# A fused agent attention and soft mixture of experts on one core: the expert layers in half tiles, with a new order of all steps

## The chip, the cores and the metric

The kernel runs on one core of a Trainium2 chip. The metric is the device time of one execution in microseconds (us), the median of several runs. A profile of one execution gives the trace that is read here; the engines in it are TensorE (PE, with its weight loads as PEld), VectorE (DVE), ScalarE (ACT), GpSimd (POOL) and the queue that issues the transfers (SP).

## The reference

Everything is float32. Attention comes first: four batches of 11456 tokens with 128 channels, and 49 agents in each batch.

```python
a2k = softmax(scale * agents @ k.T);  agent_v = a2k @ v
q2a = softmax(scale * q @ agents.T);  x = q2a @ agent_v        # 45824 x 128 over all batches
logits = x @ phi                                               # 32 slots: 8 experts x 4
d = softmax over the tokens of logits;  slot_input = d.T @ x   # 32 x 128
for e in range(8):                                             # w1: 128 x 1024, w2: 1024 x 128
    slot_out[e] = relu(slot_input[e] @ w1[e]) @ w2[e]          # 4 x 128
c = softmax over the slots of logits;  out = c @ slot_out      # 45824 x 128
```

The expert layers work on 32 rows in all, but no output can be formed before they are done, since the softmax over the tokens needs every logit.

## The kernel before

The work has three stages. In the load stage q, k and v stream in from device memory in tiles of about 1 MB (`qx`, `kx`, `kv` issue them); TensorE forms the scores (`ks`, `qs`), the agents' values (`kE`), transposes (`qp`) and logits (`ql`), and the other engines do the softmaxes. The logits of all tokens stay on the chip in `x_all`. In the middle stage the slots' inputs are completed (`ea` to `l4`), and the expert layers run (`mh`, `mr`, `mt`, `mc`, `mo`), then the sum over experts and its division (`ms`, `sb`, `sd`), which leave `sob`. In the output stage 25 chunks of the softmax over the slots are multiplied with `sob` (`oo`), copied out of the accumulators (`va` on VectorE, `vb` on ScalarE) and stored (`od`). A chunk's softmax before that is a row maximum (`cr`, VectorE), a subtraction (`cu`, GpSimd), an exponential (`ce`, ScalarE), a sum (`os`, VectorE), a small addition (`oe`, ScalarE), a reciprocal (`or`, VectorE), a product (`om`, GpSimd) and a transposition (`ot`, VectorE). These need only the logits, so they fill VectorE's time in the middle stage.

The order of all 1281 steps is one list written out by hand (`ORDER`). Each engine runs its steps in the order in which they stand in it, and the SP queue issues the transfers in that order. A step may be put anywhere behind what it depends on.

The weights `w1` (4 MB, `w10` to `w13`) and `w2` (4 MB, `w20` to `w23`) come in as eight transfers of 1 MB. Seven of them need memory that is free only once the last `kE` step (`kE23`) has read its tile; `w22` uses a buffer of the q tiles, and ORDER has it between `kv21` and `kv22`.

The first expert layer (`m_h`, L786): `si[:, e, :]` holds expert e's four slots in columns 4e to 4e+3 of 32 columns, zeros elsewhere. Experts 0 to 3 (`eh` 0) and 4 to 7 (`eh` 1) have a tile each; expert 4eh+j is written to the rows 32j to 32j+31, so that four products run side by side in four column groups of the array. Of the 32 rows of a block 4 hold values. `m_relu`, `m_trans` and `m_copy` then handle 128 x 512 for each half `fh` of each tile: four of each, 16 transposes in all. `m_out` (L816) is 64 products of 128 columns. `m_so` copies 128 x 128, and `m_sb` adds the four blocks with one product.

Of the kernel before, what the change touches and what calls it, by code (L numbers as in the profile page):

```python
# [47 lines left out]
wu qx0 qs0.0 qs0.1 kx0 ks0.0 ks0.1 qt0 qm0 qx1 qs1.0 qE0.0 qE0.1 qE0.2 km0 qs1.1 qt1 qx5 qE0.3 qm1
qu1 qs5.0 qs5.1 qt5 qm5 kz0 qw0 qr0 qx2 qs2.0 qs2.1 qt2 qm2 qe1 kb0 kr0 ke0.0 kx1 ks1.0 ks1.1 kp0
qE2.0 km1 kz1 kb1 kr1 qx3 qu5 qe5 qs3.0 qs3.1 ke0.1 kT0 kx2 ks2.0 ks2.1 qf5 kp1 qE2.1 qt3 ke1.0  # L50
ke1.1 qd1 qw1 qm3 kx3 ks3.0 qE2.2 km2 kT1 qN0 qp0.0 qp0.1 kz2 qd5 qE2.3 qc0 qw2 ks3.1 qu3 qe3 kv0
kE0 kA0 kb2 kr2 kp2 qr1 km3 kz3 qr2 ke2.0 ke2.1 kT2 ka1 qx4 qs4.0 qs4.1 qd3 qw3 kb3 qN1 qp1.0
qp1.1 kv1 kr3 kp3 kE1 qN2 ka2 qc1 kx4 ks4.0 ks4.1 ka3 ke3.0 ke3.1 qw5 qr3 qt4 qm4 qE4.0 kx5 ks5.0
kA1 km4 kz4 ks5.1 qE4.1 qE4.2 kT3 kb4 kr4 kp4 ke4.0 kv2 kE2 cx0 qp2.0 qp2.1 kv3 qN3 ke4.1 qp3.0
kA2 kT4 kE3 km5 kz5 kb5 qc2 qp3.1 kr5 am0 ka5 qx6 qs6.0 qs6.1 ke5.0 ka4 qc3 ke5.1 qr5 kA3 kv4 kE4
kv5 kT5 kE5 qx11 qs11.0 qt6 qm6 kA4 kA5 qE4.3 qw4 qr4 kg5.1 kh5.1 kg5.2 kh5.2 kg5.3 kh5.3 qs11.1
qt11 qN5 ql0 qM0 qv0 r20 qx9 qs9.0 qE6.0 qE6.1 qs9.1 qN4 qx7 qs7.0 qs7.1 kx6 qt9 r40 qp4.0 r30 qt7
qm7 qm9 qm11 qE6.2 qE6.3 qw6 r50 qp4.1 qp5.0 qc4 ks6.0 ks6.1 km6 qr6 kz6 ru0.0 qp5.1 qc5 qx8 qs8.0
qs8.1 qt8 ql1 kb6 kr6 ke6.0 ke6.1 kp6 qx10 qs10.0 qs10.1 qm8 qE8.0 qN6 kh5.4 qM1 qv1 r21 qt10
re0.0 qE8.1 ru0.1 qu9 qx12 re0.1 qs12.0 qs12.1 qt12 qE8.2 r41 r31 r51 rg0.0 kT6 kx7 ks7.0 ks7.1  # L60
km7 rg0.1 rc0 qE8.3 qe9 qw8 ru1.1 kz7 cr1 kx8 ks8.0 ks8.1 qp6.0 kb7 kr7 km8 qu7 qe7 qd7 qp6.1 kv6
kE6 qf9 qr8 kz8 ke7.0 ke7.1 qc6 kT7 qw7 qr7 ql2 kp7 kb8 kr8 ke8.0 qN8 kA6 ka7 ke8.1 re1.1 qM2
ru1.0 re1.0 r22 qm10 kx9 ks9.0 ks9.1 r42 kv7 kE7 qm12 qd9 kA7 r32 qN7 qp7.0 qv2 qp7.1 r52 kp8
rg1.0 rg1.1 km9 cr3 qE10.0 qE10.1 kz9 qc7 kv8 qp8.0 ru2.1 qp8.1 qc8 kx10 ks10.0 cu3 qx14 qw9 rc1
# [24 lines left out]
qw20 qu21 qe21 ru7.1 qf21 kE19 qE22.0 kT20 qt24 kb21 kr21 qx19 qr20 ke21.0 ke21.1 ql8 kA19 qs19.0
qs19.1 rg7.0 qd21 qM8 r28 r48 qm24 qv8 qw21 qr21 r38 kx22 kx23 ce6 kp21 qN20 ks22.0 qN21 qz17 qw23  # L90
ks22.1 re7.1 rg7.1 qt19 km22 qr18 r58 ea qE24.0 ka20 rc7 kz22 qp20.0 kT21 qE22.1 qE22.2 kE20 qN18
kA20 kb22 kr22 qm19 ks23.0 ks23.1 cr16 ru8.1 km23 kz23 kv21 ke22.0 ke22.1 kT22 qp20.1 re8.1 kp22
qu19 qc20 qe19 kE21 kb23 kr23 qd19 ke23.0 ke23.1 kT23 qp21.0 ru8.0 qw19 ka23 w22 ka21 kA21 qr19
qp21.1 qc21 cu16 qN19 cu2 cr15 kv22 ka22 qw24 kE22 cr12 kA22 kv23 qE22.3 qw22 kE23 ce4 re8.0 qr24
# [959 lines left out]
```

## Time and profile before

| | us |
|---|---|
| median of 3 runs | 287.17 |
| lowest and highest run | 286.89, 287.3 |
| the profiled execution: its own time | 286.32 |
| its span in the trace | 284.3 |

| engine | busy us | share of the span |
|---|---|---|
| PE | 243.7 | 86% |
| DVE | 221.3 | 78% |
| ACT | 198.6 | 70% |
| POOL | 126.2 | 44% |

A share of busy time is an average over stages with different limits, so the trace is read by stage. 103.82 MB are moved in the span, 79.70 MB read and 23.59 MB written.

### The profile page before, as it was taken

Reading aid. Unit: us, or ns where it says so; the run is one execution under the profiler, and the core shown is the slowest. Engines: PE = TensorE matmul, PEld = TensorE weight load, DVE = VectorE, ACT = ScalarE, POOL = GpSimd, SP = SyncE. Lnnn points to the kernel's source line nnn. Section 1 sums busy time; section 2 is a strip of 40 time slices with the busy share of each in tenths; the row PEclk is TensorE's granted clock in tenths of the full one; section 3 lists DMA queues with packets and bytes.
Section 4 is the critical chain, followed back from the end, with each engine's and each line's share of the span. In section 5 each row is a group of like instructions: output and inputs, shape, how many; then the busy total and the mean of one; then the engine's idle time right before and its main releaser. Section 6 shows DMA issues by size and latency. Waiting matters only on the chain.

```text
span 284.3 us, 8467 instructions
## 1 busy us (share of the span) xinstructions
PE 243.7 (86%) x3370; PEld 130.6 (46%) x3370; DVE 221.3 (78%) x431; ACT 198.6 (70%) x678; POOL 126.2 (44%) x139
## 2 busy tenths in 40 slices
PE   6959889999998999999999999997599878487920
PEld 4213646543564655356664556865437422122200
DVE  0597774699998878999989999988558998686510
ACT  2459696566997876599889888988713597657630
POOL 0034521207565341565752676795602868244100
PEclk9999999999999999999999999999759797668555
DMA  7999999999999999999999999379700299999996
GB/s 251 428 418 418 420 408 416 424 403 416 342 427 419 418 420 419 395 372 417 419 418 420 408 413 411 118 308 425 308 2 2 116 415 420 412 420 425 421 417 279
DMA packets 16454, 103.82 MB, mean 365 GB/s; under 512 B 2080, under 2 KB 2464, under 8 KB 5152
## 3 DMA queue, kind: packets, MB, share of 16 engines
q1 hardware_dynamic: 16272, 103.21, 89.0%
q8 instruction: 26, 0.43, 0.6%
q10 hardware_dynamic: 144, 0.08, 0.1%
q14 instruction: 12, 0.10, 0.1%
HBM read 79.70 MB, written 23.59 MB: 363 GB/s over the span
## 4 chain that ended last, share of the span: by engine, by line
PE 52%; DMA 28%; DVE 8%; ACT 4%; issue 3%; SPq 1%; ACTq 1%; DVEq 0%
PE ev L313 12%; PE sq L236 12%; DMA qt<-qT 10%; DMA out<-ot 10%; PE sk L236 9%; PE tp L470 6%; DMA vt<-vL 4%; DMA kt<-kT 3%; ACT ot L877 3%; PE gp L577 3%; PE lq L520 3%; PE pa L864 2%; PE hp L790 2%; DVE ct L856 1%; DVE cd L838 1%
## 5 line engine op out<-in xcount | busy, mean ns | idle before, releaser
L438 ACT ACTIVATE pt<-pt,mx 128x49 f32<-128x49 f32 x148 | 47.5, 326 | 0.1
L236 PE MATMUL sk<-kt,ag 128*32 128x512 f32 (+1 forms) x384 | 45.8, 570 | 1.6 <-DMA kt<-kT 1.4
L236 PE MATMUL sq<-qt,ag 128*32 128x512 f32 (+3 forms) x400 | 43.8, 554 | 3.8 <-DMA qt<-qT 3.6
L313 PE MATMUL ev<-vt,et 128*64 128x129 f32 x720 | 44.9, 276 | 2.1 <-DMA vt<-vL 1.4
L864 PE MATMUL pa<-ct,sob 32*128 32x512 f32 (+2 forms) x50 | 35.0, 824 | 11.5 <-DVE ct L856 8.0
L877 ACT COPY ot<-pb 128x1536 f32<-128x1536 f32 (+2 forms) x25 | 32.4, 1307 | 17.4 <-DMA out<-ot 9.9
L313 PEld LDWEIGHTS ev<-vt,et 128*64 128x64 f32 x720 | 39.3, 136 | 8.9 <-issue 6.2
L459 POOL TENSOR_TENSOR pt<-pt,rt 128x784 f32<-128x784 f32 (+3 forms) x20 | 27.1, 1355 | 34.6 <-DVE rt L455 26.5
L296 ACT ACTIVATE es<-sk,nm 128x512 f32<-128x512 f32 (+1 forms) x48 | 29.7, 652 | 10.3 <-DVE nm L287 8.2
L864 PE MATMUL pb<-ct,sob 32*128 32x512 f32 (+2 forms) x150 | 36.1, 834 | 0.0
L850 POOL TENSOR_TENSOR x_all<-x_all,cd 128x512 f32<-128x512 f32 (+2 forms) x25 | 23.6, 961 | 24.9 <-DVE cd L845 24.6
L553 POOL TENSOR_TENSOR dt<-x_all,mb 128x512 f32<-128x512 f32 (+1 forms) x20 | 24.2, 1217 | 21.5 <-DVE mb L549 17.7
L306 DVE STREAM_TRANSPOSE et<-es 128x1024 f32<-128x1024 f32 (+1 forms) x24 | 28.0, 1165 | 3.1 <-ACT es L296 3.1
L589 POOL TENSOR_TENSOR x_all<-x_all,r_all 128x512 f32<-128x512 f32 (+3 forms) x25 | 23.8, 963 | 14.1 <-DVE r_all L585 8.5
L475 ACT COPY pT<-tp 128x1024 f32<-128x1024 f32 (+3 forms) x25 | 23.0, 920 | 8.8 <-PE tp L470 8.8
L268 DVE TENSOR_REDUCE mt<-sk 128x2 f32<-128x1024 f32 (+1 forms) x24 | 27.4, 1141 | 1.8 <-PE sk L236 1.5
L438 ACT ACTIVATION_READ_ACCUMULATOR pt<-pt,mx 128x1 f32 x148 | 28.0, 189 | 0.0
L864 PEld LDWEIGHTS pa<-ct,sob 32*128 32x128 f32 x50 | 10.2, 246 | 33.7 <-DVE ct L856 22.1
L874 DVE COPY ot<-pa 128x512 f32<-128x512 f32 (+2 forms) x25 | 15.5, 624 | 12.9 <-DMA out<-ot 9.5
L413 DVE STREAM_TRANSPOSE pt<-sq 128x1024 f32<-128x1024 f32 (+3 forms) x20 | 21.9, 1097 | 2.0 <-PE sq L236 1.5
L236 PEld LDWEIGHTS sq<-qt,ag 128*32 128x32 f32 x400 | 10.9, 109 | 23.4 <-issue 16.7
L470 PE MATMUL tp<-cs,pt 128*128 128x128 f32 x140 | 21.3, 283 | 0.0
(126 smaller groups left out, 421.6 us busy)
## 6 DMA issues: line engine op xcount, KB each, us to landing
out<-ot SPq DMA_DIRECT2D x21, 1024.0 KB, 7.2
vt<-vL SPq DMA_DIRECT2D x20, 1032.0 KB, 11.1
qt<-qT SPq DMA_DIRECT2D x20, 1024.0 KB, 9.4
kt<-kT SPq DMA_DIRECT2D x19, 1024.0 KB, 9.3
w2s<-w SPq DMA_DIRECT2D x4, 1024.0 KB, 9.4
w1s<-w SPq DMA_DIRECT2D x4, 1024.0 KB, 15.1
vt<-vL SPq DMA_DIRECT2D x4, 645.0 KB, 8.3
kt<-kT SPq DMA_DIRECT2D x4, 640.0 KB, 9.1
```

The source lines that it names most:

```text
L236: t_.matmul(sp[32 * q4:32 * q4 + 32, h, :nt], ag[:, b, 32 * h:32 * h + 32], xv[:, q4, :], start=True, stop=True)
L268: v_.tensor_reduce(out=k["mt"][:, 0:2], in_=k["s"][:, :, :nt], axis=AX.X, op=ALU.max, negate=True)
L296: s_.activation(out=k["e"][:, h, :nt], in_=k["s"][:, h, :nt], func=AF.Exp, bias=k["nm"][:, 2 * h:2 * h + 1])
L306: v_.transpose(out=k["et"][:, :n].rearrange("p t (h a) -> p h t a", h=2), in_=k["e"][:, :, :nt].rearrange("p h (t a) -> p h t a", a=32))
L313: t_.matmul(k["ev"][o:o + AW, :], k["et"][:, c, :], k["v"][:, c, :], start=c < 2, stop=c >= n - 2)
L438: s_.activation(out=x, in_=x, func=AF.Exp, bias=q["mx"][:, c:c + 1], accum_out=q["rt"][:, c:c + 1])
L459: g_.tensor_tensor(out=x, in0=x, op=ALU.mult, in1=q["rt"][:, :n].unsqueeze(2).to_broadcast([P, n, A]))
L470: t_.transpose(q["tp"][:, h, j % 4, :], q["pt"][:, 2 * j:2 * j + 2, :].rearrange("p c a -> p (c a)"), ident)
L553: g_.tensor_tensor(out=q["dt"][:, :q["n"]], in0=x_all[:, q["at"]:q["at"] + q["n"]], op=ALU.add, in1=r["mb"].unsqueeze(1).to_broadcast([P, ...
L589: g_.tensor_tensor(out=x_all[:, x], in0=x_all[:, x], op=ALU.subtract, in1=r_all[:, x].unsqueeze(2).to_broadcast([P, q["n"], S]))
L864: t_.matmul(pb[:, r - 1, :32 * n] if r else pa[:, :32 * n], sob[32 * r:32 * r + 32, :], z["ct", j][32 * r:32 * r + 32, :32 * n], start=Tru ...
L877: s_.copy(out=o_ov(j)[:, 1:4], in_=z["pb", j][:, :, :32 * CHUNKS[j]])
```

## The change

All eight experts now go into one tile, in two column ranges of 512 (`fh`) that are taken in quarters of 256 columns (`q`): for each j expert j and expert j+4 are added up in the same 32 rows, where they sit in different rows. Relu, transposes and copies are made on 128 x 256 four times, and there are 8 transposes. In the second layer one product has 256 columns: the second-layer weights of experts j and j+4 side by side. Each row is right in one of the two halves; two masks `sel_e`, made by two ScalarE instructions in `am0`, select it in `m_sb`, which becomes two products. The weights' layout in device memory is changed to match, and `w1`'s two first pieces are all that `mh0` needs, its two last `mh1`. And ORDER is written anew for all steps; what follows shows its stretch around the expert layers.

```diff
 ORDER = """
...
-kA23 os3 qr22 qp18.0 qp18.1 kg23.2 qN24 qN22 kg23.1 kh23.1 os0 kh23.2 qr23 kh23.4 w20 qp19.0 qN23
-rg8.0 eb oe3 kg23.3 kh23.3 qc18 os7 cr13 cr14 cr17 os1 rg8.1 rc8 or3 os2 qp19.1 qc19 oe0 ql10 w21
-w23 cu14 w11 w13 qM10 r210 qp24.0 ec qc24 cu15 ce15 ed ql9 r410 r310 qM9 r29 or0 rx10 ry10.0
-qp22.0 qp22.1 qc22 cu7 cu11 ef r49 r39 eg ce2 ce14 oe2 qv9 ql12 rg10.0 eh qp23.0 r59 ru9.1 cu13
-ry10.1 rg10.1 ru9.0 qz24 om3 ei oe7 qc23 qM12 ce16 r212 os4 oe1 r412 r312 rx12 ql11 or2 qv12 qM11
-r211 r411 r311 nm os8 rc10 re9.1 ce11 re9.0 rx11 dE ej wt rg9.0 rg9.1 rc9 ry11.0 ry11.1 or7 wr ws
-ce10 rg11.0 rg11.1 f0 ry12.0 rc11 rg12.0 rc12 gm qv10 cu17 om2 cu12 ce12 ce13 ce17 l1 l2 ce9 f1 l3
-cr24 f2 l4 os17 ce7 d1 qv11 os9 w10 mh0.0 mh0.1 mr0.0 cr21 cu24 w12 mh1.0 mh1.1 mr1.0 or1 os6 os5
-cu8 mt0.0 mr0.1 mt0.1 oe4 om1 ce24 mr1.1 mt1.0 mt1.1 oe8 mc0.0 om0 ot0 mo0.0 oe5 mc0.1 mc1.0 mc1.1
-d2 cr18 mo0.1 cr19 mo1.0 or4 os14 ot1 or5 ot2 ot3 mo1.1 ms oe6 cu19 ce8 os11 om7 d3 d4 sb sd oo0
...
+kz22 kT21 qs19.1 rg7.0 kb22 kr22 ke22.0 kp22 qE22.1 ka22 rg7.1 ce8 rc7 ks23.0 ea qt19 qm19 kE20
+r58 kA20 cu7 qf21 ke22.1 kv22 qd21 qN20 qN18 ks23.1 qp18.0 qp18.1 kv21 kE21 cr14 km23 kz23 qE22.2
+qw21 kb23 kT22 qr21 ru8.1 kr23 qd23 qu19 ce2 kA21 cr15 qp20.0 qe19 kE22 ke23.0 ke23.1 qN21 kT23
+kv23 kE23 cr12 ka23 qp20.1 qd19 qE22.3 kA22 re8.1 ce6 kA23 ru8.0 qw19 qr19 os0 w11 re8.0 qp21.0
+os3 cr13 qc20 qr24 os5 qw23 kg23.1 rg8.0 rg8.1 qw22 qr22 qr23 os1 kh23.1 rc8 qp21.1 qc21 kg23.3
+kg23.2 kh23.2 kh23.3 qN19 qp19.0 qp19.1 cu15 kh23.4 qN24 qc18 eb ql10 qc19 qp24.0 ec os2 oe3 qc24
+qN22 oe1 qN23 os8 os4 ql9 qM10 r210 r410 ed os7 qp22.0 r310 rx10 qp22.1 qM9 oe2 qc22 ef eg r29 r49
+cu10 ry10.0 or1 qp23.0 qc23 oe8 ry10.1 rg10.0 rg10.1 r39 cu12 ce7 eh qv9 cu13 ce13 r59 ru9.1 ei
+cr16 os10 ql11 qM11 ce12 oe7 rc10 ql12 qM12 r212 r412 r211 cr18 os14 ce9 r312 ru9.0 qz24 r411 r311
+cr19 ce11 re9.0 re9.1 oe0 rx11 rg9.0 nm wt wr oe5 os6 rg9.1 rx12 ry11.0 qv12 ws rc9 oe4 ry11.1
+rg11.0 rg11.1 or8 ry12.0 or5 rg12.0 os11 or2 oe6 cu14 cu16 om8 w12 w20 w21 ce16 rc11 f0 rc12 om1
+om2 oe14 or14 gm l1 f1 or0 om0 l2 or6 w13 om6 cu19 oe11 f2 l3 l4 ce15 ce14 qv10 dE ce10 w23 or4
+qv11 w10 mh0.0 mh0.1 mr0.0 mh1.0 mr0.1 mt0.0 om14 mt0.1 ej mc0.0 cr24 os12 or3 mh1.1 ce19 or7
+mc0.1 d1 mo0 mr1.0 mr1.1 os16 mt1.0 mt1.1 cu18 ot0 cr20 cu20 mc1.0 mc1.1 mo1 os13 w22 mo2 mo3 d2
+ot1 ot2 om5 d3 cr21 cu21 cu24 oe10 ms sb d4 oe13 sd oo0 va0 ce24 om3 ot3 oe16 vb0 od0 os9 oe9 oo1
...
-    so = keep.tile([P, C], F32, name="so")
+    so = keep.tile([P, 2, C], F32, name="so")
+    sel_e = keep.tile([P, 2, P], F32, name="sel_e")
...
     def am():
         s_.mul(out=ag[:, 1:], in_=ag[:, 1:], mul=SCALE)
+        for h in range(2):
+            s_.activation(out=sel_e[:, h], in_=sel_d, func=AF.Copy,
+                          scale=cs[:, CO_EM + h:CO_EM + h + 1])
...
+    def m_h(fh, q):
+        if q == 0:
+            hps[fh] = tile_("s", [P, 2, 512], f"hp_{fh}")
+        for e in range(E):
+            j = e % 4
+            t_.matmul(hps[fh][32 * j:32 * j + 32, q, :256], si[:, e, :],
+                      z["w1"][:, 2 * fh + e // 4, j, q * 256:q * 256 + 256],
+                      start=e < 4, stop=e >= 4)
+
+    def m_relu(fh, q):
+        if q == 0:
+            hss[fh] = tile_("pt", [P, 2, 512], f"hs_{fh}")
+            v_.tensor_scalar(out=hss[fh][:, 0, :256], in0=hps[fh][:, 0, :256], scalar1=0.0,
+                             scalar2=None, op0=ALU.max)
         else:
-            s_.activation(out=hss[eh][:, 1], in_=hps[eh][:, 1], func=AF.Relu)
+            s_.activation(out=hss[fh][:, 1, :256], in_=hps[fh][:, 1, :256], func=AF.Relu)
+
+    def m_trans(fh, q):
+        if q == 0:
+            htp[fh] = tile_("s", [P, 2, 4, P], f"htp_{fh}")
+        for i in range(2):
+            t_.transpose(htp[fh][:, q, i, :], hss[fh][:, q, i * P:(i + 1) * P], ident)
+
+    def m_copy(fh, q):
+        if q == 0:
+            hts[fh] = tile_("pt", [P, 2, 4, P], f"ht_{fh}")
+            s_.copy(out=hts[fh][:, 0, 0:2], in_=htp[fh][:, 0, 0:2])
         else:
-            v_.tensor_copy(out=hts[eh][:, 1], in_=htp[eh][:, 1])
+            v_.tensor_copy(out=hts[fh][:, 1, 0:2], in_=htp[fh][:, 1, 0:2])
+
+    def m_out(x):
+        if not x:
+            z["so"] = tile_("a", [P, 2, C], "so_p")
+        for i in range(2):
             for j in range(4):
+                t_.matmul(z["so"][32 * j:32 * j + 32],
+                          hts[x // 2][:, x % 2, i, 32 * j:32 * j + 32],
+                          w2s[x][:, i, 2 * j:2 * j + 2, :], start=not x + i,
+                          stop=x == 3 and i == 1)
...
     def m_sb():
         z["sb"] = tile_("a", [P, C], "sb_p")
-        t_.matmul(z["sb"], sel_d, so, start=True, stop=True)
+        for h in range(2):
+            t_.matmul(z["sb"], sel_e[:, h], so[:, h], start=not h, stop=h == 1)
...
+        h[fh] = [op("mh", (fh, q), "P", lambda fh=fh, q=q: m_h(fh, q),
+                    deps=[si4] + wx[2 * fh:2 * fh + 2] + ([("mh", fh, 0)] if q else []),
...
+        r = [op("mr", (fh, q), "A" if q else "V", lambda fh=fh, q=q: m_relu(fh, q),
+                deps=h[fh] + ([("mr", fh, 0)] if q else []),
...
+        t[fh] = [op("mt", (fh, q), "P", lambda fh=fh, q=q: m_trans(fh, q),
+                    deps=r + ([("mt", fh, 0)] if q else []),
...
```

The transfers are issued by the new list in the order `kv22 kv21 kv23 w11 w12 w20 w21 w13 w23 w10 w22`; by the old one in the order `kv21 w22 kv22 kv23 w20 w21 w23 w11 w13 w10 w12`.

## Rows read from the trace of the kernel before

**Rows 1.** The page: DMA share in 40 slices of 7.1 us; instruction queue (packets, MB, share)
```profile
DMA  7999999999999999999999999379700299999996
...
q8 instruction: 26, 0.43, 0.6%
```

**Rows 2.** Windows by stage; the header names the columns
```profile
core 0: us, PE busy (x) PEld busy (x) DVE busy (x) ACT busy (x) POOL busy (x), PEclk, DMA share, GB/s
0.00:52.60 52.60, 43.91 (x478) 24.02 (x478) 33.63 (x57) 32.53 (x134) 12.26 (x17) 1.00 0.98 396
52.60:185.00 132.40, 130.27 (x2102) 72.37 (x2103) 121.19 (x223) 109.02 (x444) 70.83 (x73) 1.00 0.97 392
185.00:207.70 22.70, 17.56 (x411) 12.83 (x411) 17.06 (x49) 16.75 (x44) 15.44 (x21) 0.88 0.80 326
207.70:221.80 14.10, 12.59 (x180) 7.00 (x180) 11.06 (x28) 3.56 (x11) 3.54 (x5) 0.82 0.01 2
221.80:284.30 62.50, 39.37 (x200) 14.37 (x200) 38.38 (x79) 36.77 (x47) 24.17 (x25) 0.67 0.92 378
```

**Rows 3.** Timeline of the SP queue, 160 to 200 us: start, duration, line, transfer
```profile
184.99 1.28 SPq L683 DMA_DIRECT2D w2s<-w  x3
186.31 2.33 SPq L678 DMA_DIRECT2D w1s<-w  x4
```

**Rows 4.** The chain that ended last, 203 to 224 us: start, duration, what
```profile
204.14 2.16 issue
206.30 0.63 PE fb L745 x2
...
207.53 0.20 DVE si L765
...
207.77 6.10 PE hp L790 x32
...
213.90 0.69 DVE hs L797
...
216.06 1.23 DVE ht L814 x2
...
220.62 0.18 DVE so L827
...
221.45 0.35 DVE sob L834
```

**Rows 5.** Windows of one us, columns as in rows 2
```profile
205.00:206.00 1.00, 0.00 (x0) 0.00 (x0) 0.00 (x0) 1.00 (x2) 1.00 (x2) 0.50 0.08 33
...
211.00:212.00 1.00, 1.00 (x8) 0.20 (x4) 0.52 (x1) 0.00 (x0) 0.00 (x0) 0.50 0.00 0
212.00:213.00 1.00, 1.00 (x12) 0.32 (x8) 0.77 (x2) 0.79 (x3) 0.00 (x0) 0.66 0.00 0
```

**Rows 6.** Groups by shape, 207 to 222 us: count, busy us, mean ns, idle before
```profile
L838 DVE TENSOR_REDUCE cd<-x_all 128x16 f32<-128x512 f32 x6 | 3.8, 654 | 0.0
L822 PE MATMUL so_p<-w2s,ht 128*32 128x128 f32 x128 | 3.7, 273 | 0.0
...
L806 PE MATMUL htp<-cs,hs 128*128 128x128 f32 x16 | 2.2, 281 | 0.0
...
L797 DVE TENSOR_SCALAR hs<-hp 128x512 f32<-128x512 f32 x2 | 1.4, 692 | 2.9 <-PE hp L790 2.9
L814 DVE COPY ht<-htp 128x512 f32<-128x512 f32 x2 | 1.3, 672 | 0.0
...
L800 ACT ACTIVATE hs<-hp 128x512 f32<-128x512 f32 x2 | 1.2, 597 | 7.7 <-DVE hs L797 7.7
...
L831 PE MATMUL sb_p<-so,cs 128*128 128x128 f32 x2 | 0.5, 326 | 1.0 <-DVE so L827 1.0
...
L827 DVE COPY so<-so_p 128x128 f32<-128x128 f32 x1 | 0.2, 240 | 0.0
```

**Rows 7.** Timeline of VectorE, 183 to 224 us: one transposition of logits
```profile
202.77 1.21 DVE L532 STREAM_TRANSPOSE x_all<-lq 128x1024 f32<-128x1024 f32 x1
```

More of the change, by code (lines that the diff above doesn't have):

```diff
@@ L44 @@
 CO_AB = CO_DD + P
-CO_N = CO_AB + P
+CO_EM = CO_AB + P
+CO_N = CO_EM + 2
 ORDER = """
[L48 to L64, printed above, removed]
@@ L89 @@
[L89 to L94, printed above, removed]
@@ new lines @@
+qp2.0 kv1 qE0.2 qE0.3 qu3 qe3 kp2 kE1 qp2.1 km3 kz3 qw0 qf5 qd5 ke2.1 kT2 qr0 qc2 kb3 qm4 qw1
+qE4.0 kA1 kx4 kr3 kp3 ks4.0 ks4.1 km4 kx5 ks5.0 ks5.1 qN0 kz4 kb4 kr4 ke3.0 kv2 qr1 kE2 ke3.1 kT3
+kp4 cx0 qp0.0 qp0.1 qw5 km5 kA2 kz5 ke4.0 ke4.1 ka4 qN1 qp1.0 kT4 qE4.1 qd3 qw3 ka3 qc0 kv3 kE3
+kA3 qp1.1 kb5 kv4 kE4 qc1 qr3 qx6 kr5 ke5.0 ke5.1 kT5 kA4 kv5 qx11 qN3 qp3.0 am0 qs6.0 qs6.1 kE5
+ka5 qE4.2 qE4.3 qw4 qr4 kA5 qt6 qp3.1 kg5.1 kh5.1 kg5.2 kh5.2 qc3 qs11.0 kg5.3 kh5.3 qm6 qE6.0
+qE6.1 qE6.2 qN4 qs11.1 qt11 ql0 qM0 qx9 r20 qv0 qs9.0 qs9.1 qt9 r40 kx6 ks6.0 r30 qm9 r50 ks6.1
@@ L676, in z_w1 @@
         if "w1" not in z:
-            z["w1"] = wl("w1s", [P, E, F])
-        nc.sync.dma_start(out=z["w1"][:, 2 * x:2 * x + 2, :], in_=w1[x])
+            z["w1"] = wl("w1s", [P, 4, 4, F // 2])
+        nc.sync.dma_start(out=z["w1"][:, x], in_=w1[x])
     def z_w2(x):
-        w2s[x] = (tile_("qt", [P, 2, F // P, C], f"w2s{x}") if x else
-                  wl(f"w2s{x}", [P, 2, F // P, C]))
+        w2s[x] = (tile_("qt", [P, 2, E, C], f"w2s{x}") if x else
+                  wl(f"w2s{x}", [P, 2, E, C]))
         nc.sync.dma_start(out=w2s[x], in_=w2[x])
@@ L784, in z_d4 @@
         s_.copy(out=dr, in_=z["dr"])
-    def m_h(eh, fh):
-        if fh == 0:
-            hps[eh] = tile_("s", [P, 2, 512], f"hp_{eh}")
-        for j in range(4):
-            t_.matmul(hps[eh][32 * j:32 * j + 32, fh, :], si[:, 4 * eh + j, :],
-                      z["w1"][:, 4 * eh + j, fh * 512:fh * 512 + 512], start=True, stop=True)
-    def m_relu(eh, fh):
-        if fh == 0:
-            hss[eh] = tile_("pt", [P, 2, 512], f"hs_{eh}")
-        if fh == 0:
-            v_.tensor_scalar(out=hss[eh][:, 0], in0=hps[eh][:, 0], scalar1=0.0, scalar2=None,
-                             op0=ALU.max)
-        else:
-            s_.activation(out=hss[eh][:, 1], in_=hps[eh][:, 1], func=AF.Relu)
@@ L802, in m_trans @@
-    def m_trans(eh, fh):
-        if fh == 0:
-            htp[eh] = tile_("s", [P, 2, 4, P], f"htp_{eh}")
-        for i in range(4):
-            t_.transpose(htp[eh][:, fh, i, :], hss[eh][:, fh, i * P:(i + 1) * P], ident)
-    def m_copy(eh, fh):
-        if fh == 0:
-            hts[eh] = tile_("pt", [P, 2, 4, P], f"ht_{eh}")
-        if fh == 0:
-            s_.copy(out=hts[eh][:, 0], in_=htp[eh][:, 0])
-        else:
-            v_.tensor_copy(out=hts[eh][:, 1], in_=htp[eh][:, 1])
-    def m_out(eh, fh):
-        if not eh and not fh:
-            z["so"] = tile_("a", [P, C], "so_p")
-        for f in range(4):
+    def m_h(fh, q):
[6 more added lines that the diff above has]
+                      start=e < 4, stop=e >= 4)
@@ L920, in tile_agent_attn_soft_moe @@
     d4 = op("d4", (), "A", z_d4, deps=(d3,), gives=(("a", d3),))
-    mo = None
-    for eh in range(2):
-        h = [op("mh", (eh, fh), "P", lambda eh=eh, fh=fh: m_h(eh, fh),
-                deps=[si4] + wx[2 * eh:2 * eh + 2] + ([("mh", eh, 0)] if fh else []),
-                takes=() if fh else ("s",)) for fh in range(2)]
-        r = [op("mr", (eh, fh), "A" if fh else "V", lambda eh=eh, fh=fh: m_relu(eh, fh),
-                deps=h + ([("mr", eh, 0)] if fh else []),
-                takes=() if fh else ("pt",), gives=(("s", h[0]),)) for fh in range(2)]
-        t = [op("mt", (eh, fh), "P", lambda eh=eh, fh=fh: m_trans(eh, fh),
-                deps=[r[fh]] + ([("mt", eh, 0)] if fh else []),
-                takes=() if fh else ("s",), gives=(("pt", r[0]),)) for fh in range(2)]
-        c = [op("mc", (eh, fh), "V" if fh else "A", lambda eh=eh, fh=fh: m_copy(eh, fh),
-                deps=t + ([("mc", eh, 0)] if fh else []),
-                takes=() if fh else ("pt",), gives=(("s", t[0]),)) for fh in range(2)]
-        for fh in range(2):
-            mo = op("mo", (eh, fh), "P", lambda eh=eh, fh=fh: m_out(eh, fh),
-                    deps=[c[fh]] + wy[2 * eh:2 * eh + 2] + ([mo] if mo else []),
-                    takes=() if eh + fh else ("a",), gives=(("pt", c[0]),))
@@ L940, in tile_agent_attn_soft_moe @@
-    ms = op("ms", (), "V", m_so, deps=(mo,), gives=(("a", ("mo", 0, 0)),))
+    h, t, c = {}, {}, {}
+    for fh in range(2):
+        h[fh] = [op("mh", (fh, q), "P", lambda fh=fh, q=q: m_h(fh, q),
+                    deps=[si4] + wx[2 * fh:2 * fh + 2] + ([("mh", fh, 0)] if q else []),
+                    takes=() if q else ("s",)) for q in range(2)]
+        r = [op("mr", (fh, q), "A" if q else "V", lambda fh=fh, q=q: m_relu(fh, q),
+                deps=h[fh] + ([("mr", fh, 0)] if q else []),
+                takes=() if q else ("pt",), gives=(("s", h[fh][0]),)) for q in range(2)]
+        t[fh] = [op("mt", (fh, q), "P", lambda fh=fh, q=q: m_trans(fh, q),
+                    deps=r + ([("mt", fh, 0)] if q else []),
+                    takes=() if q else ("s",), gives=(("pt", r[0]),)) for q in range(2)]
+        c[fh] = [op("mc", (fh, q), "V" if q else "A", lambda fh=fh, q=q: m_copy(fh, q),
+                    deps=t[fh] + ([("mc", fh, 0)] if q else []),
+                    takes=() if q else ("pt",), gives=(("s", t[fh][0]),)) for q in range(2)]
@@ L941, in tile_agent_attn_soft_moe @@
+    mo = None
+    for x in range(4):
+        mo = op("mo", (x,), "P", lambda x=x: m_out(x),
+                deps=c[x // 2] + [wy[x], ("am", 0)] + ([mo] if mo else []),
+                takes=() if x else ("a",), gives=(("pt", c[x // 2][0]),))
+    ms = op("ms", (), "V", m_so, deps=(mo,), gives=(("a", ("mo", 0)),))
     b0 = op("sb", (), "P", m_sb, deps=(ms,), takes=("a",))
@@ L1019, in _constants @@
     c[:, CO_DD:CO_DD + P] = p[:, None] % S == p[None, :] % S
+    for h in range(2):
+        c[:, CO_EM + h] = p % S // SE == 4 * h + p // 32
     return c
```

90 lines of the change are left out of this document (50 added, 40 removed).

## The prediction, made before the changed kernel ran

> **What bounds the kernel now.** I read the page's slices first, then the windows by stage, then the chain of waits around the expert layers. The slices show DMA full in the load stage and again at the end, with holes around 180 us and between 204 and 225 us [rows 1]. The windows say why the holes count [rows 2]. From 52.6 to 185.0 TensorE is busy 130.27 of 132.40 us while DMA moves 392 GB/s: both are nearly full, and TensorE has 2.1 us to give. From 221.8 on the stores run at 378 GB/s over the stretch, ramp and tail included, so this stage's length is set by bytes that do not change. Whatever lies between, from the last `kE` step (185.0) to `sob` (221.8), delays the first store and so the end, one for one. That is 36.8 us, of which DMA uses some 19 for the seven weight transfers issued from 184.99 on [rows 3].
>
> In this middle part the chain of waits goes through a wait of TensorE at 204.14 that the profile calls issue (2.16 us), the products `fb`, `si_p` and then `hp` (6.10 us), and from 213.9 almost only VectorE: `hs`, `ht`, `so`, `sob`, with reductions of the output stage's chunks in between [rows 4]. The second layer's products (3.7 us) and the transposes (2.2 us) are busy time of TensorE [rows 6], but the chain does not run through them. So what they save is worth little; what VectorE saves between `si` and `sob` counts. From 207.73, the end of `si`, to 221.80, the end of `sob`, it takes 14.07 us.
>
> **The change part by part.** The sum is made against the profiled execution, 286.32 us, which is 0.85 below the median of 287.17; I add that at the end.
>
> *Load stage.* Nothing in it is computed differently. Two ScalarE instructions of 128 columns in `am0` come on top, beside a TensorE that bounds. `w22` (1.05 MB) moves from this stage to the end of the weights, which relieves a DMA that is not alone in bounding. One `qp` half more than before stands behind `kE23`, not ahead of it, which cancels. The rest is the new order, which I can bound only: below by TensorE's 2.1 us of idle time [rows 2], above by one transfer that arrives a place too late, 1.05 MB at 392 GB/s or 2.7 us. I take 0, since the slack on either side is small: near the stage's end I followed in the new list `kv21` (its buffer is free after `kE19`, and some ten steps of TensorE stand between that and `kE21`) and `kv23` (free after `kE20`), and found both covered.
>
> *From `kE23` to `si`.* Three things.
> (a) All eight weights now start behind `kE23`. Seven were issued from 184.99 on and in by 205 [rows 3, 5], at most 2.9 us each; at 392 GB/s it is 2.7. `w10`, which `hp` needs, is seventh and would land 19 to 20 us behind `kE23`; `hp` began 22.8 behind it. `w22` lands 22 to 23 behind it and is needed by `mo2`, some 8 us after `hp` begins. Both are hidden; if `hp` came 3 us earlier, `w10` would be the next to wait for.
> (b) VectorE gets more filler ahead of `l4`: five sums and three maxima of 16 cells net of shared ones, 0.65 each [rows 6], and five reciprocals, put at 0.2 (under the 0.24 of `so`); it loses two maxima (1.1), a transposition of logits (1.2 [rows 7]) and four small ones (0.8). Net 3.1 us. VectorE was idle 22.70 − 17.06 = 5.6 us there [rows 2]. It fits, if the idle places are where the filler stands. I take 0, bounds 0 and +3.1.
> (c) The wait of 2.16 us. TensorE waits for no engine [rows 4]; yet with the weights landed 33 GB/s still move in 205 to 206 us [rows 5], and an instruction queue moved 0.43 MB in 26 packets, so 16.5 KB each [rows 1]. I read it as TensorE waiting for its next block of instructions. Then its place is a count of instructions. `dE` (three products, so six records and six weight loads) moves from ahead of `rg9` to behind `l3`; the wait would fall 12 instructions later, past `fb` and `si_p` (eight [rows 4]) and into `dE`. `f2` and `l4` then run under it, and `hp` follows the wait by 0.2 and not by 1.47 us, a gain of 1.3. Against it, `w22` keeps DMA busy 2.7 us longer, and the block may arrive later. Bounds −2.2 (no wait) and 0; I take −0.8, nearer to the 1.3.
> The Trainium skill (Runtime: NRT & Kernel Launch, Instruction fetch mechanics) says that an engine's instructions are fetched in 16 KiB blocks while the one before runs, and that a boundary's cost is mostly hidden. The packet size agrees with the row; the 2.16 us, if they are this, do not agree. By the page there would be nothing to pay here, and the sum below would be 1.4 us lower.
>
> *From `si` to `sob`.* TensorE's work for the first layer is the same (32 products of 256 columns for 16 of 512, four side by side). It starts at the lower clock level again: the granted clock was 0.50 until 212 and 0.66 in 212 to 213 us [rows 5], 4.9 us after `hp` began, so a quarter of `hp` takes 1.75 us, and 0.9 after that. An `hs` or `ht` of 256 columns on VectorE is put between 0.24 (128 columns) and 0.69 (512): 0.39 [rows 6]; on ScalarE 0.40, between half and all of 0.60. Times after `si`:
> - three quarters of `hp` end at 1.75, 3.5 and 5.2; the first two `hs`, VectorE then ScalarE, at 4.6;
> - four transposes at 0.14 each (2.2/16): 5.8; their copies, ScalarE then VectorE: 6.6; the last quarter of `hp`: 6.7;
> - its `hs` pair: 7.6; four transposes: 8.2. VectorE has two reductions and an `ot` in its queue meanwhile, until 8.8; its `ht`: 9.2;
> - then on VectorE a reduction (0.65), the three small instructions of `d2` (put at 0.15 each), two `ot` of 128 and 256 columns (0.24 and 0.39, as the copies) and a reduction, 2.4 in all: 11.6. `mo2` and `mo3`, half of the 3.7 us, end at 11.1 under this cover; without it they would set `so` at 11.2;
> - `so`, now 256 columns, 0.39: 12.0; `sb`, two products for one of 0.49: 12.75; `sob` 0.35 and its start: 13.2.
> Against 14.07 that is −0.9. Bounds: 0, if the filler takes up what is saved; −2.5, if all of VectorE's relief is on the chain (1.0 from the halves less the wider `so`, and four reductions fewer, 2.6, less 1.1 for other moves).
>
> *Output stage.* Same chunks, same bytes. Ahead of the first three stores VectorE has filler of the same length within one reduction: 0, bounds −0.65 and +0.65.
>
> Sum: 0 + 0 − 0.8 − 0.9 + 0 = −1.7, so 284.6 for an execution like the profiled one, and **285.5** against the median.
>
> **The rivals.**
> 1. The wait at `fb` is gone. For it: nothing else in the load stage shows so long a one; against: the burst of small products ahead of it, `rg9` to `rg12`, is unchanged. −2.2 − 0.9 = −3.1: 284.1.
> 2. Slower: VectorE becomes the bound ahead of `si`. The place is `l2` and `l4`, queued behind `os11`, `cr19`, `os14` and the others; all of the 3.1 us on the chain gives −1.7 + 3.1: 288.6. It turns the sign once more than 1.7 us of the filler stands where VectorE had no idle time. For it: VectorE is 17 of 22.7 us busy already; against: 2.2 of its 5.6 idle us lie under the wait before `fb` [rows 4], and the filler can use them.
> 3. Slower: one tile of the load stage comes late for TensorE, 2.7 us in a stage where TensorE has nothing else to do: −1.7 + 2.7: 288.2.
> 4. No change: TensorE's savings were never on the chain, and VectorE's are taken up by the moved filler. 287.2.
>
> **How the numbers follow.** A measurement of this kernel can tell about 0.2% (0.6 us) from no change. Chances: forecast 0.42, rival 1 0.20, rival 2 0.15, rival 3 0.11, rival 4 0.12. Faster is the forecast and rival 1, 0.62; same is rival 4, 0.12; slower is rivals 2 and 3, 0.26. The forecast's own range is 284.6 to 286.4. The range for 8 in 10 takes in most of rival 1 and of rivals 2 and 3: 283.5 to 288.4.
>
> **What would show it.** In the profile after: the end of `kE23` near 185.0 (load stage right); an issue wait of TensorE behind `si_p` and not before `fb`; VectorE's idle time ahead of `l4` smaller by some 3 us, with `hp` starting no later than 22 us behind `kE23`; `hs` and `ht` near 0.39; 13.2 us from `si` to `sob`; DMA full from the first stores to the end. I am wrong if `kE23` ends more than 1 us off, if `l4` waits in VectorE's queue with its product done, or if `so` waits on TensorE.

## The result, and the profile after

The changed kernel takes 290.27 us (median of 4, 288.30 to 291.72) beside 287.03 us (286.14 to 287.30) of the kernel before on the same chip: a ratio of 1.0113 with a 95% interval of 1.0068 to 1.0157. It is slower by 1.1%; 285.5 us and a gain were forecast. The profiled execution took 289.74 us, its span is 288.0, 3.7 more than before. Ratios, here and below, leave out executions over 1.5% above the fastest one of the same kernel.

The windows of the changed kernel, with the columns of [rows 2]. The first cut is at 52.60 us as there (`kE5` ends then in the kernel before, and at 53.3 in the changed one); the others are at the same three events (the end of `kE23`, the end of `si`, the end of `sob`):

```profile
0.00:52.60 52.60, 44.45 (x466) 23.11 (x468) 31.73 (x54) 32.14 (x135) 11.28 (x15) 1.00 0.97 390
52.60:188.17 135.57, 131.10 (x2116) 72.30 (x2113) 123.28 (x222) 110.36 (x445) 72.12 (x76) 1.00 0.94 378
188.17:210.90 22.73, 18.67 (x408) 14.22 (x408) 19.89 (x59) 17.71 (x49) 16.27 (x20) 0.84 0.92 371
210.90:225.17 14.27, 12.93 (x149) 6.75 (x149) 8.91 (x24) 2.48 (x9) 6.64 (x9) 0.77 0.01 3
225.17:288.00 62.83, 37.61 (x200) 13.58 (x200) 36.48 (x75) 36.27 (x44) 20.14 (x21) 0.74 0.91 376
```

Against [rows 2] the load stage is 3.2 us longer (135.57 for 132.40), and TensorE's idle time in it has grown from 2.1 to 4.5 us, while DMA fell from 392 to 378 GB/s: TensorE and the DMA engines both wait more than before. The other three stretches differ by 0.0, +0.2 and +0.3. So in these two profiles the loss is the load stage; what follows it nets nothing. TensorE is also busy 0.8 us longer in it, with 14 records more (and 12 fewer in the stretch before; a product is two records, a transposition one). The page's rate by slices of 7.2 us, up to 180 us and after the first slice, is lowest in the 13th (289 GB/s), where TensorE is idle for 1.4 of 8 us and was for 1.0 before, and in the 17th to 19th (379, 385 and 353; 115 to 137 us), to which I come below.

The chain of the changed kernel through the middle, which answers to [rows 4]:

```profile
209.46 0.56 PE fb L750 x2
210.02 0.56 PE si_p L767 x2
210.59 0.14 PE de_p L720
210.72 0.65 issue
211.38 0.42 PE de_p L720 x5
211.80 5.28 PE hp L796 x48
...
223.60 0.34 DVE so L832
...
224.81 0.36 DVE sob L840
```

The issue wait stands where the prediction put it, behind `si_p` and within `dE`. But it ends at 211.38, 23.2 us behind `kE23`; before it ended at 206.30, 21.3 behind [rows 3, 4]. So `hp` starts 23.6 us behind `kE23` for 22.8 before: a loss of 0.8 where a gain of 0.8 was forecast. From the start of `hp` to the end of `sob` it is 13.4 us for 14.0. The span's 3.7 us are 3.2 + 0.8 − 0.6 + 0.3.

The groups by shape of the changed kernel, 210 to 226 us, which answer to [rows 6]:

```profile
L826 PE MATMUL so_p<-w2s,ht 128*32 128x256 f32 x64 | 3.9, 382 | 0.0
...
L819 DVE COPY ht<-htp 128x256 f32<-128x256 f32 x2 | 0.9, 426 | 1.6 <-ACT ht L817 1.6
L803 DVE TENSOR_SCALAR hs<-hp 128x256 f32<-128x256 f32 x2 | 0.8, 425 | 2.8 <-PE hp L796 2.8
```

`hs` and `ht` take 0.43 us on VectorE for the 0.39 of the estimate; the 64 records of 256 columns cost as much (3.9 us) as the 128 of 128 did (3.7).

**Where the load stage loses it.** The SP queue around the place, start, duration, line, transfer. First the kernel before, then the changed one:

```profile
123.71 0.33 SPq L230 DMA_DIRECT2D kt<-kT  x1
124.08 0.82 SPq L259 DMA_DIRECT2D vt<-vL  x1
128.67 0.33 SPq L230 DMA_DIRECT2D kt<-kT  x1
```

```profile
124.92 0.33 SPq L232 DMA_DIRECT2D kt<-kT  x1
125.29 0.43 SPq L261 DMA_DIRECT2D vt<-vL  x1
130.55 0.33 SPq L232 DMA_DIRECT2D kt<-kT  x1
130.92 0.43 SPq L261 DMA_DIRECT2D vt<-vL  x1
```

In the old list the order is `kv14 kx17 kv15 kx18 kv16`, in the new one `kx17 kv14 kx18 kv15`. So the transfer `kv15` is the second row before (124.08) and the last row after (130.92). `kx18` needs a k buffer that the scores `ks16` still read, and the queue issues in its order: `kv15`, whose buffer has long been free, stands behind that wait. The chain of the changed kernel shows it link by link:

```profile
128.57 1.96 PE sk L238 x16
...
130.55 0.33 SPq L232
...
130.92 9.13 DMA vt<-vL
...
140.18 1.99 PE ev L315 x32
```

The scores end at 130.53, `kx18` goes at 130.55, `kv15` behind it at 130.92, and its tile is in at 140.05, when TensorE has run out of other work. Windows of 4 us, the kernel before and then the changed one:

```profile
134.00:138.00 4.00, 4.00 (x66) 2.80 (x66) 3.73 (x9) 3.54 (x10) 2.90 (x4) 1.00 1.02 426
138.00:142.00 4.00, 4.00 (x50) 2.24 (x44) 3.81 (x9) 3.46 (x14) 3.62 (x4) 1.00 1.00 414
```

```profile
134.00:138.00 4.00, 3.44 (x60) 2.18 (x60) 3.21 (x7) 4.00 (x14) 4.00 (x6) 1.00 0.99 375
138.00:142.00 4.00, 3.06 (x44) 2.19 (x36) 2.58 (x4) 3.29 (x20) 2.82 (x3) 1.00 1.01 410
```

TensorE is idle for 1.5 of these 8 us, and for another 0.5 in 126 to 130: 2.0 of the 2.4 us by which its idle time grew.

### The profile page after: what moved, and what is told of

It is laid out like the page before. It is cut to its first block, busy times and chain, and to the rows that moved or that the text cites. A ratio compares the mean times of both kernels' runs of the same rounds, so it can differ in the third digit from the quotient of the medians.

```text
span 288.0 us, 8390 instructions
## 1 busy us (share of the span) xinstructions
PE 244.8 (85%) x3332; PEld 130.0 (45%) x3332; DVE 220.3 (77%) x431; ACT 199.0 (69%) x680; POOL 126.4 (44%) x139
## 4 chain that ended last, share of the span: by engine, by line
PE 50%; DMA 30%; DVE 8%; ACT 3%; issue 3%; SPq 2%; POOL 1%; DVEq 0%; ACTq 0%
PE sk L238 11%; DMA kt<-kT 10%; PE ev L315 10%; DMA vt<-vL 10%; PE sq L238 9%; DMA out<-ot 8%; PE tp L472 5%; PE gp L579 3%; PE pa L870 3%; PE lq L522 3%; PE hp L796 2%; ACT ot L883 2%; DMA w1s<-w 2%; DVE ct L862 1%; DVE ot L880 1%
## 5 line engine op out<-in xcount | busy, mean ns | idle before, releaser
L238 PE MATMUL sk<-kt,ag 128*32 128x512 f32 (+1 forms) x384 | 46.4, 570 | 3.4 <-DMA kt<-kT 2.2
L238 PE MATMUL sq<-qt,ag 128*32 128x512 f32 (+3 forms) x400 | 45.7, 554 | 2.7 <-DMA qt<-qT 2.7
L870 PE MATMUL pa<-ct,sob 32*128 32x512 f32 (+2 forms) x50 | 31.4, 739 | 12.7 <-DVE ct L862 9.5
L870 PE MATMUL pb<-ct,sob 32*128 32x512 f32 (+2 forms) x150 | 32.8, 753 | 0.0
L856 POOL TENSOR_TENSOR x_all<-x_all,cd 128x512 f32<-128x512 f32 (+2 forms) x25 | 23.6, 962 | 20.4 <-DVE cd L851 16.0
L425 POOL TENSOR_TENSOR pt<-pt,mx 128x784 f32<-128x784 f32 (+2 forms) x10 | 12.9, 1288 | 31.5 <-DVE mx L420 29.5
L870 PEld LDWEIGHTS pa<-ct,sob 32*128 32x128 f32 x50 | 9.4, 228 | 33.6 <-DVE ct L862 22.0
## 6 DMA issues: line engine op xcount, KB each, us to landing
w2s<-w SPq DMA_DIRECT2D x4, 1024.0 KB, 14.1
```

Source lines behind the costliest of these rows:

```text
L238: t_.matmul(sp[32 * q4:32 * q4 + 32, h, :nt], ag[:, b, 32 * h:32 * h + 32], xv[:, q4, :], start=True, stop=True)
L870: t_.matmul(pb[:, r - 1, :32 * n] if r else pa[:, :32 * n], sob[32 * r:32 * r + 32, :], z["ct", j][32 * r:32 * r + 32, :32 * n], start=Tru ...
```

## The experiments

Three theories of the loss: **the load stage** (two v tiles are issued late in the new order); **the wait** (TensorE's issue wait, by its place or by when it ends); **the layers** (the new expert layers themselves are slower). Ratios are to the kernel before on the same chip, with their 95% intervals; each kernel had 6 to 12 executions, that before 17 to 29.

**Halves of the change.** The first has the changed code with the old order up to `kE23` and the new one behind it; the second the new order with the old layers; the third the new layers in the old order (only `mr` and `mo` are placed anew):

```diff
-cu8 mt0.0 mr0.1 mt0.1 ... mo0.0 oe5 mc0.1 mc1.0 mc1.1 d2 cr18 mo0.1 cr19 mo1.0 ... mo1.1
+cu8 mr0.1 mt0.0 mt0.1 ... oe5 mc0.1 mo0 mc1.0 mc1.1 d2 cr18 mo1 cr19 mo2 ... mo3
```

> The changed kernel, with the steps up to kE23 in the old order (without w22, which stays last) and the rest in the new. Theory A (the new order of the load stage costs 3.2 us, the rest follows it one for one): kE23 ends near 185.0 instead of 188.2, and the time falls by about 3.2 from the changed kernel, to about 287. Rival B (the load stage is late for another reason that stays here: w22 gone from it, or the two mask instructions in am0): kE23 still near 188, time near 290.

> The kernel before, its layers and weight layout unchanged, with the new order of all steps. Theory A: kE23 near 188, si to sob not shorter than in the kernel before; the time is that of the changed kernel or up to 1 us above it, 290 to 291. Rival C (the layers' change itself makes the loss): near 287.

> The changed layers, masks and weight layout in the old order; only the ScalarE relu of the first half moves ahead of the first transposes and the first second-layer products behind both copies, as the new dependencies ask. Theory A: kE23 near 185, the wait before fb stays, si to sob 0.5 to 1 us shorter: 286 to 286.7, faster by 0.1 to 0.3%. Rival C: slower than 287.

Measured: 1.0083 (1.0049 to 1.0116), 1.0086 (1.0052 to 1.0121) and 0.9990 (0.9961 to 1.0019). The theory of the layers falls: alone they change nothing that can be told, and the order alone loses most of it (288.87 us, under the 290 to 291 expected). The first was meant to show that the load stage is the whole loss, and failed for a reason of its own. `kE23` ends at 185.75, so the load stage is mended; but the two orders don't fit at their seam, and `hp` starts 26.6 us behind `kE23`. Its chain there:

```profile
185.90 2.71 POOL x_all L590 x3
...
188.63 1.15 ACT x_all L595 x2
189.78 0.53 ACT dt L570
...
190.35 1.26 PE gp L578 x52
```

A step whose tile TensorE needs (`dt`) stands on ScalarE behind two exponentials, which wait for GpSimd's subtractions. So its time says nothing on either of the other two theories.

**The two v tiles.** In the changed kernel `kv14` and `kv15` are moved ahead of `kx17` and `kx18`; and in the kernel before the two k tiles are moved ahead of the v tiles, and nothing else:

```diff
-kz16 qt18 qm17 kx17 kv14 kE14 ... ke16.1 kx18 ks18.0 ... ka16 kv15 kE15
+kz16 qt18 qm17 kv14 kx17 kE14 ... ke16.1 kv15 kx18 ks18.0 ... ka16 kE15
```

> The changed kernel with two transfers moved: kv14 ahead of kx17 and kv15 ahead of kx18, as the old order has them. Theory A2 (the loss of the load stage is made at one place: kv15 stands in the SP queue behind kx18, which waits for the scores that read its buffer, so kE15 waits for its tile): TensorE has no wait of its own kind between 130 and 142 us, kE17's group ends 2 to 3 us earlier against TensorE's work ahead of it, kE23 ends near 186, time 287 to 288. Rival E (the loss is spread over the stage, or falls due at the next late tile): kE23 stays near 188 and the time near 290.

> The kernel before, with two transfers moved: kx17 ahead of kv14 and kx18 ahead of kv15, as the new order has them. Theory A2: kE15 waits for its tile, kE23 ends 1.5 to 3 us later, time 288 to 289.5. Rival E: no change, within 0.5 us.

Measured: 1.0034 (0.9997 to 1.0071) and 1.0110 (1.0054 to 1.0166). The place takes 0.8% from the changed kernel when it is mended, and puts 1.1% on the kernel before when it is planted there. So the times show from both sides that the place of these two transfers costs about this much. In the mended kernel `kv15` is issued at 123.27 and `kE23` ends at 185.7. The profiled execution of the planted one was its fastest (286.16 us, median 288.60), and still has the hole, in a stage where before had none:

```profile
134.00:138.00 4.00, 2.29 (x38) 1.46 (x32) 4.00 (x8) 2.67 (x7) 2.57 (x4) 1.00 1.02 421
```

How the place turns into time the traces show only in part. In this planted execution `kE23` ends at 185.9, 0.9 us later than before for the 1.5 to 3 expected, and the eight kernels that keep the old order up to there (`w22` aside) have it anywhere from 184.5 to 185.8, against 188.2 in the changed kernel and 186.9 in the one with its order and the old layers. And the mended kernel was expected to have no wait between 130 and 142 us, but TensorE waits there for the k tile `kx18`:

```profile
136.40 1.06 PE L237 MATMUL sk<-kt,ag 128*32 128x512 f32 x8 [1.35 <-DMA kt<-kT]
```

From 124 to 144 us it is idle for 1.6 us, against 0.0 in the kernel before, 2.0 in the changed one and 2.0 in the planted one. What else the mend saves, one profile of each kernel does not tell: the larger part of the 1.9 us by which TensorE's idle time up to `kE23` fell lies at 82 to 98 us, ahead of the edit (1.4 and 0.4 us; the kernels with the old order have 0.5 to 1.9 there).

**w22.** The new layers in the old order, with `w22` moved from the load stage to the end of the weights, as the change has it; and the mended kernel with `w22` put back into the load stage:

```diff
-ru8.0 qw19 ka23 w22 ka21 ... cr21 cu24 w12 mh1.0
+ru8.0 qw19 ka23 ka21 ... cr21 cu24 w12 w22 mh1.0
```

```diff
-qp18.0 qp18.1 kv21 kE21 ... mc1.1 mo1 os13 w22 mo2
+qp18.0 qp18.1 kv21 w22 kE21 ... mc1.1 mo1 os13 mo2
```

> The changed layers in the old order, with w22 moved from the load stage to the end of the weights. If moving w22 costs nothing (the prediction): the same as with it early, 285.8 within 0.6. If the hole in DMA ahead of the weights is the price, up to 2.5 us slower; if the load stage gains by it, up to 2.5 us faster.

> The changed kernel with the two v tiles issued ahead of the two k tiles in the load stage, as in the experiment before, and with w22 issued between kv21 and kE21, about where the kernel before has it, instead of last of the weights. Theory (w22 as the last of eight weights makes TensorE's instruction wait end about 1 us later): with seven weights behind kE23 the wait in or near dE ends 0.8 to 1.2 us earlier, hp starts that much earlier, and the ratio falls from 1.003 to about 0.999 (0.997 to 1.001). Rival (w22 in the load stage takes 2.7 us of DMA time there and makes a late tile later by as much as it gives): kE23 ends 0.5 to 1.5 us later, and the ratio stays at 1.003 (1.001 to 1.005).

Measured: 1.0032 (1.0003 to 1.0062), 0.4% above the same kernel without the move; and 1.0004 (0.9972 to 1.0035), 0.3% under its own. In both pairs the intervals overlap, so `w22`'s price is only likely: both say 0.3 to 0.4%. With both repairs the changed kernel is level with the kernel before. TensorE waits for none of `w22`'s data. What grows is the wait for instructions, as TensorE's timeline has it in the kernel with `w22` last (start, duration, idle time before in brackets; 2.32 without the move):

```profile
207.56 0.63 PE L749 MATMUL fb<-fd,sel_on 32*128 32x32 f32 x2 [3.29 <-issue]
```

But there the wait also begins earlier: it ends 21.9 us behind `kE23` for 21.7 without the move, which does not account for 0.4%. In the mended kernel the step is larger. With `w22` early no wait is left, all six records of `dE` stand together, and `hp` starts 22.4 us behind `kE23` for 23.7:

```profile
207.78 0.47 PE L719 MATMUL de_p<-cs,gt 50*32 50x1 f32 x6
208.19 5.35 PE L795 MATMUL hp<-w1s,si 128*32 128x256 f32 x48
```

**The place of the wait.** In the changed kernel `dE` is moved back ahead of `rg9`; in the new layers with the old order, and in the kernel before with nothing else changed, it is moved behind `l3`; and in the second of these `d1` goes behind `mh1.1`:

```diff
-rx11 dE ej wt rg9.0 ... l3 cr24 f2 l4 ... mh0.1 mr0.0 cr21
+rx11 wt rg9.0 ... l3 cr24 f2 dE l4 ... mh0.1 mr0.0 ej cr21
```

> The changed kernel with dE back ahead of rg9.0 and its copy ej behind nm. Theory A: the load stage stays late; TensorE's wait (0.65 us in the changed kernel) falls ahead of fb or si_p again or vanishes, dE's own 0.4 us leave the way of hp, so hp comes up to 1 us earlier behind kE23 and the time falls by 0.4 to 1. Rival D: the wait grows to 2 us again once it is at fb, and nothing or up to 1 us is lost.

> The changed layers in the old order, with dE moved from ahead of rg9.0 to behind l3 and its copy ej behind mr0.0. Theory F (the wait of 2.2 us falls after a fixed count of TensorE's instructions): it appears behind si_p, l4 runs under it, hp comes 0.5 to 1.3 us earlier and the time falls by as much. Rival G (it belongs to fb): it stays before fb, nothing is gained and dE's 0.4 us come on top.

> The kernel before, with its expert layers unchanged, and only dE moved behind f2 (on TensorE behind l3) and ej behind mr0.0. Theory (the wait's place is a count of instructions, and this move alone puts fb and si_p ahead of it): the wait of 2.2 us falls behind si_p into dE, hp starts 0.8 to 1.3 us earlier behind kE23 than before, and the ratio is 0.9955 to 0.998; it then lies 0.0005 to 0.002 above the experiment that has the new layers too, since those were worth some 0.1 per cent. Rival (the gain of that experiment came from the new layers, which need their input earlier): the ratio is 0.999 to 1.001 although the wait has moved.

> The fastest kernel so far (new layers in the old order, dE behind f2) with d1, a step of three small VectorE instructions, moved from behind l4 to behind mh1.1. Theory (hp now waits for nothing but si, and d1 stands beside it on VectorE, not ahead of it): no change that can be told, 0.9955 to 0.998. Rival (d1 delays the first relu or the reductions that fill behind it): 0.25 us less, ratio 0.995 to 0.9965.

Measured: 1.0143 (1.0096 to 1.0190); 0.9968 (0.9939 to 0.9997); 0.9960 (0.9935 to 0.9985); 0.9944 (0.9912 to 0.9975). With `dE` ahead the kernel is not faster by the 0.4 to 1 us expected. The wait is 1.98 us and falls among the last records of `gt_p`. The profile names a ScalarE step as what ended it, but that step was done 0.57 us before, and a packet of the instruction queue started 2.7 us before (212.0), as at the other waits (last section), so I read it as the wait for instructions. The time says little, since the interval meets that of the changed kernel and the profiled load stage was another 3.3 us longer. With `dE` behind, the wait falls into `dE` in all three others: 1.25, 1.63 and 1.06 us. TensorE's timeline of the kernel before with that one move, beside [rows 4]:

```profile
205.12 0.41 PE L761 MATMUL si_p<-gt,av 49*128 49x32 f32 x2
205.45 0.22 PE L714 MATMUL de_p<-cs,gt 50*32 50x1 f32 x2
207.30 0.37 PE L714 MATMUL de_p<-cs,gt 50*32 50x1 f32 x4 [1.63 <-issue]
```

`hp` starts 21.9 us behind `kE23` for 22.8, and the kernel gains 0.4%: the theory's own range, and the rival (that the layers are needed for it) falls. It lies 0.1% below the one with the new layers, not above it as expected, which the intervals don't tell apart. The move of `d1` was not expected to show; the kernel came out 0.2% faster, below both ranges, but the intervals overlap here too.

**What the wait waits for.** The last kernel takes the fastest one and starts two of the seven weights later, held by two small copies of a value that is ready late:

```diff
-ql10 w21 w23 cu14 w11 w13 qM10 ... f1 l3 ... os9 w10 mh0.0 ... w12 mh1.0
+ql10 cu14 w11 w13 w10 w12 qM10 ... f1 w21 w23 l3 ... os9 mh0.0 ... mh1.0
+        if x % 2:
+            s_.copy(out=w2s[x][0:S, 0, 0, 0:S], in_=fd)
```

> The fastest kernel so far (new layers in the old order, dE behind f2, d1 behind mh1.1) with five weight transfers behind kE23 instead of seven: w21 and w23, which the second layer needs last, start only when f0 is done some 15 us later, held by two small ScalarE copies of fd into their tiles; w10 and w12 stand ahead of them. Theory (TensorE's instruction wait ends some 2 us after the burst of weights behind kE23 ends, since its block comes through the same DMA engines): the five are in about 5 us earlier, the block arrives before TensorE needs it, the issue wait of 1.1 us in de_p is gone, hp starts some 20.2 us behind kE23 instead of 21.2, and the ratio is 0.989 to 0.993. Rival A (the wait belongs to the place and not to the traffic, so it stays): ratio 0.994 to 0.996. Rival B (the late two make the next block late, or arrive late for the second layer): an issue wait or a DMA wait ahead of or within so_p, up to 2 us, ratio 0.995 to 1.002.

Measured: 0.9871 (0.9830 to 0.9912). A single low execution (279.61 us) makes this ratio rest on six of twelve; the medians of all are 283.74 and 285.99, a ratio of 0.992. So the gain over the kernel before is 0.8 to 1.3%, and that over the fastest kernel until then 0.1 to 0.7%, which the medians don't tell from nothing. The profile decides on the mechanism: the window of one us at 200, then TensorE's timeline.

```profile
200.00:201.00 1.00, 0.66 (x45) 0.61 (x49) 0.85 (x3) 1.00 (x3) 0.94 (x2) 1.00 0.18 74
```

```profile
205.64 0.47 PE L721 MATMUL de_p<-cs,gt 50*32 50x1 f32 x6
206.05 6.48 PE L797 MATMUL hp<-w1s,si 128*32 128x256 f32 x64
```

The five weights are in at 200, no wait is left in `dE`, and `hp` starts 20.3 us behind `kE23`, as expected. Neither late weight holds `so_p`, which begins at 213.86 as the transposes end. By this trace rivals A and B fall, and by its median this is the fastest version made here.

## Why the prediction was wrong

**The load stage (failed).** "The rest is the new order, which I can bound only ... I take 0, since the slack on either side is small" is the step that failed. The term measured +3.2 us in the profile; by the ratios, 0.8% (2.3 us) of it goes when two v tiles are put back. Its upper bound (one transfer a place too late, 2.7 us) and the third rival named the right thing, at 0.11; the place was readable in the new list. I followed `kv21` and `kv23`, the last two of 24 v tiles, and took them for the rest. What had to be asked of every transfer is what stands ahead of it in the queue and what that waits for. With TensorE busy 130.27 of 132.40 us [rows 2] there is slack for neither side of such a place: the planted edit moves two transfers past two others and costs 1.1%. That such a place costs time is shown by the edits; how much of it is TensorE's idle time there is open.

**`w22` (failed in its price).** "Both are hidden" was right of the data and wrong of the time. The sentence in (c), that the block may arrive later since `w22` keeps DMA busy 2.7 us longer, was the right one, but I priced it inside an interval that ended at 0. Measured: the wait ends 1.9 us later behind `kE23` than before, of which moving `w22` back returns 1.2 us at `hp`; in time it is 0.3 to 0.4%, not clear of noise.

**The wait (c).** Its place was right: 10 instructions later by the records (12 where the old order is kept), past `fb` and `si_p`, into `dE`. Its term was +0.8 for −0.8. `w22` accounts for a part: with it early again `hp` starts 22.4 us behind `kE23`, not 23.6. The filler below accounts for more: in that kernel no wait is left, and `hp` still gains only 0.4 us on the kernel before, as `si` ends at 22.3. In the old order the move of `dE` alone gains 0.9 us and 0.4%. The first rival (no wait at all) came true in three kernels: that one, the last one, and the first half of the change, where TensorE reached the place 3 us later.

**VectorE's filler (b) (failed, and hidden).** It came to 19.89 − 17.06 = 2.8 us for the 3.1 estimated, but "I take 0" does not hold. `si` ends 22.6 us behind `kE23` for 22.7 before, which looks free; but before, 2.16 us of wait lay ahead of `si`, and now the wait lies behind it. Where the wait is moved and the old order kept (four kernels), `si` ends 20.0 to 20.2 us behind `kE23`; with the new order in this stretch (four kernels, without the one with the bad seam and the one with `dE` ahead) 22.0 to 22.6. So the new order takes 1.8 to 2.6 us of what the move of `dE` gives. Some 0.8 us of it is filler on the chain, between a product of VectorE (`rz`) and a maximum (`m_all`) that TensorE waits for; `r_all` and `cd` are the filler. The chain of the changed kernel, then that of the kernel before:

```profile
202.32 0.23 DVE rz L539 x2
202.55 0.59 DVE r_all L587
203.15 0.59 DVE cd L844
203.74 0.15 DVE m_all L547 x2
```

```profile
198.59 0.17 DVE rz L537
...
199.20 0.17 DVE m_all L545
```

What makes the rest, these runs do not show. The second rival was right of the mechanism, at another place than it named; the later wait for instructions covers most of its price in the changed kernel.

**From `si` to `sob`.** Counted from `hp`, 13.4 us against the 13.2 forecast (which had `hp` start with `si`'s end) and 14.0 before. The size looks right, but one trace cannot carry it: from `hp` to `sob` the four profiles with the old layers have 13.0 to 14.0 us, those with the new layers 12.6 to 14.1, since the granted clock during `hp` differs. By the ratios the layers give 0.1% (0.9990) or cost 0.1% (0.9968 against 0.9960 with `dE` moved): nothing that these runs can tell, where −0.9 us would be 0.3%. The fourth rival (no change) was right of this part.

**Output stage:** +0.3, within its bounds.

## What to carry to other kernels

A new order of a queue that issues in order is read by asking of each transfer whose buffer is free: what stands ahead of it, and what is that waiting for? Two such places among some seventy transfers cost more here (0.8 to 1.1%) than the layers gave (nothing that can be told). A step taken for a price of nothing needs every instance followed, or a chance as large as its bound.

Work that "nobody waits for" can still hold TensorE: traffic delays its instructions. Where a burst of small products meets a burst of transfers, send what is needed late, late. And where a wait is moved, ask what stood under it: filler that was free beside the wait is on the chain without it.
